# An adaLN transformer block on one Trainium2 core: one transfer for a slot in attention, SyncE in source order and residual rows loaded later in the feed-forward

## The chip, the cores and the metric

The kernel runs on one core of one Trainium2 chip. The metric is the device time of one execution in microseconds (us). Five engines with queues of their own work side by side: TensorE (PE, matrix products; PEld is its loading of weights), VectorE (DVE), ScalarE (ACT), GpSimd (POOL) and SyncE (SP, which here issues nearly all transfers and computes nothing). An engine takes the instructions of its queue in their order; between engines, semaphores make one wait for another. A transfer is carried out by the DMA engines and is behind the engine that issued it only in that this engine first waits until the transfer may start.

## The reference

One block of a transformer for 2048 rows of 512 fp32 numbers: attention with 32 query heads and 8 key heads of 128 over the last 512 keys of a cache, then a gated feed-forward of width 1792. Six vectors that come from one small product with the condition `c` shift, scale and gate both halves.

```python
def _A_ref(x, k_cache, v_cache, wq, wo):
    ...
    q = (x @ wq) ...                       # 32 heads of 128
    k = jnp.repeat(k_cache[:, :, Sk - W:, :], rep, axis=1)   # W = 512, rep = 4
    v = jnp.repeat(v_cache[:, :, Sk - W:, :], rep, axis=1)
    scores = jnp.einsum("bhqd,bhkd->bhqk", q, k) * (Dh ** -0.5)
    p = _softmax(scores, axis=-1)
    o = jnp.einsum("bhqk,bhkd->bhqd", p, v)
    return o ... @ wo

def _B_ref(x, w_gate, w_up, w_down):
    return (_gelu(x @ w_gate) * (x @ w_up)) @ w_down

mod = (_silu(c) @ w_mod).reshape(c.shape[0], 6, 1, -1)
...
h = _layernorm(x, axis=-1) * (1 + ca) + sa
x = x + ga * _A_ref(h, A_k_cache, A_v_cache, A_wq, A_wo)
h = _layernorm(x, axis=-1) * (1 + cb) + sb
x = x + gb * _B_ref(h, B_w_gate, B_w_up, B_w_down)
```

## The kernel before

**Arithmetic.** Every large fp32 product is made of three fp16 matmuls (`mm3`, L85 to L88): each operand is split into a high and a low fp16 tile, and low times high, high times low and high times high add up in one PSUM bank. The query projection and the feed-forward's first products are also done with seven block products in place of eight, so they read sums and differences of blocks of the input (the "combined blocks", loaded as `cb`) and of the weights. A set of such weights is four tiles, `w0`, `w1`, `w2` and `x3`.

**Attention** is written as a loop over T = 512 slots of 128 queries by 512 keys of one head. Four slots are a unit, sixteen a pair of heads (a group `g`, which starts at slot `t0`). Half 0, the first 256 slots, does query blocks 0 and 1 for all sixteen pairs, half 1 blocks 2 and 3. In a slot `t` TensorE makes the scores, VectorE their maximum (`peak`), ScalarE the exponentials (`expo`, L884); two slots later ScalarE writes the high part of the probabilities into a tile `p` (`high`, L896), three slots later VectorE the low part (`low`, L901), and `low` then has SyncE issue a DMA transpose of that tile (L905) into `pt`, which the product with `v` reads. There are four tiles `p` and three `pt`. Between these, TensorE works off a list of other tasks, three for each slot: query projections, products with `v`, and output rows `y`, which VectorE adds to one of eight accumulator tiles `acc` in SBUF (L852).

**Weights.** In half 0 the split tiles of `wq`, `k`, `v` and `wo` are made from raw fp32 loads, for the most part by GpSimd; each made tile is written to DRAM (`store`) and fetched again in half 1 (`fetch`, L315; both use DRAM tiles named `kept`). Half 1 prepares the feed-forward's weights in the same way, in staged tiles (`stage`) that share the five raw buffers (`prep_set`, `prep_wd`), and stores those for the feed-forward. Loads of raw tiles go through a list (`sched`): each has the slot in which its data is first used, is issued three slots earlier, and not before the buffer that it takes was released. The `xs` loads bring rows for the layer norm (raw buffers too; after attention these are the finished rows `y`), two `rw` buffers hold raw feed-forward weights.

**What sets the order.** The attention part, L1383 on, stands under `tc.manual_schedule()`: all engines keep the order of the source. At the end of a slot come `run(t)` (what was put at this slot: stores, fetches, reloads of accumulators), `run(("l", t))` (raw loads) and `run(("w", t))` (steps on loaded tiles). In before, the fetches of half 1 have fixed slots, four for a weight set at `t0 - 18` to `t0 - 15`, `k` at `t0 - 9`, `v` at `t0 + 1`, `wo` at `t0 + 12` and every second slot on. A transfer whose buffer is not yet free holds up SyncE and everything behind it, transposes included. `attn_final` (L858) stores a finished row and reloads its accumulator three slots later.

The feed-forward (L1437 on) runs over 28 chunks `q` of seven block products each, in the order 1, 2, 6, 7, 5, 4, 3; output rows `y` of the chunks before are worked in between (`y_next`). In before no manual order holds there: the framework's scheduler orders the instructions of each engine, SyncE's among them, by its own model of their durations. `f_final` (L1473) stores a row of the output and reloads the same accumulator at once for the row eight further on:

```python
def f_final(ti):
    nc.sync.dma_start(rows_of(out, ti), acc[ti])
    if ti < 2 * QT:
        load_acc(ti + 2 * QT, y1[ti + 2 * QT])
```

Of the kernel before, what the change touches and what calls it, by code (L numbers as in the profile page):

```python
# [63 lines left out]
def block_kernel(ctx: ExitStack, tc: tile.TileContext, x, kT, v, wq, wo, wg, wu, wd, cT, wc, wm, out):  # L64
# [35 lines left out]
    nc.sync.dma_start(cts, cT)  # L100
    for i in range(QT):
        load_acc(i, rows_of(x, i), nc.scalar if i < 2 else nc.sync)
# [32 lines left out]
    def mod_load(j, dt):  # L135
        t = raw("wmc")
        nc.sync.dma_start(t, wc[j, :, dt, :])
        return lambda: mod_col(j, dt, t, sbc)
# [171 lines left out]
    def store(key, t):  # L310
        KEPT[key] = dram.tile(list(t.shape), F16, name="kept")
        nc.sync.dma_start(KEPT[key], t)

    def fetch(key, t):
        nc.sync.dma_start(t, KEPT[key])  # L315
        return t
# [72 lines left out]
    def ln_out(qb, dt):  # L389
# [11 lines left out]
        def affine(act=True):  # L401
# [5 lines left out]
            nc.sync.dma_start(spilled(0, qb)[:, dt, :], st["f"])  # L407
# [12 lines left out]
    def ln_tile(gen, i, src):  # L420
# [4 lines left out]
        def load():  # L425
            st["x"] = raw("xs")
            nc.sync.dma_start(st["x"], src())
# [13 lines left out]
        def affine(dts):  # L441
# [7 lines left out]
            if KT - 1 in dts:  # L449
                nc.sync.dma_start(spilled(gen, qb)[:, :, i * P:(i + 1) * P], f.rearrange("p (k q) -> p k q", k=KT))  # L450
# [15 lines left out]
    def combos(gen, p, eng, base=True, d=0, e=0):  # L466
        X = {}

        def load(name):
# [5 lines left out]
            nc.sync.dma_start(X[name], stored(gen, name, p))  # L475
# [54 lines left out]
    def reader(src):  # L530
        st = {}

        def load():
            st["r"] = raw("raw")
            nc.sync.dma_start(st["r"], src)

        return st, load

    def wo_items(qd, ts_, tp):
        m = {}  # L540
        for k in range(4):
# [15 lines left out]
            if qd == 0:  # L557
                def load_kept(st=st, sp=sp, src=src):
                    st["r"] = sp["r"] = pool.tile([P, D], F32, tag="wo", name="wor", bufs=8)
                    nc.sync.dma_start(st["r"], src)  # L560
# [121 lines left out]
    def set_load(key, srcs, only=None):  # L682
        for k, src in enumerate(srcs):
            if only in (None, k):
                t = pool.tile([P, 512], F32, tag="rw", name="rw", bufs=NRW)
                nc.sync.dma_start(t, src)
# [224 lines left out]
    def early_load(j, dt):  # L911
        nc.sync.dma_start(wct[j][:, dt, :], wc[1, :, dt, :] if j else wm[0, dt])
# [132 lines left out]
    def gate_load(dt):  # L1045
        gps[dt] = raw("wmr")
        nc.sync.dma_start(gps[dt], wm[1, dt])
# [53 lines left out]
    for g in range(NG):  # L1101
# [136 lines left out]
    def prep_set(q, b):  # L1238
# [11 lines left out]
        def keep_it(k):  # L1250
            return lambda: store(("w", key, k), outs[k][0]["t"] if k < 3 else outs[k][0]["t"][:, :, 0:256])
# [25 lines left out]
    def prep_wd(n, b):  # L1277
# [3 lines left out]
        def load(k):  # L1281
            st[k] = raw("raw")
            nc.sync.dma_start(st[k], wd[(2 * n + k) * P:(2 * n + k + 1) * P, :])
# [19 lines left out]
        for k in range(2):  # L1303
            sched(b + 7 + 2 * k, (outs[k][1], [lambda k=k: make(k), lambda k=k: store(("wd", n, k), outs[k][0]["t"])]), b + 10 + 2 * k)
# [77 lines left out]

    with tc.manual_schedule():  # L1383
        begin()
        nexty = []
        for t in range(T + TAIL):
# [30 lines left out]
            run(("l", t))  # L1417
            run(("w", t))
            if t == T + 2:
# [23 lines left out]

    def y_next():
        if nexty:
            all_of(nexty.pop(0))

# [25 lines left out]
    def f_final(ti):  # L1473
        nc.sync.dma_start(rows_of(out, ti), acc[ti])
        if ti < 2 * QT:
            load_acc(ti + 2 * QT, y1[ti + 2 * QT])

    f_done = {(0, k) for k in ORDER} | {(1, 1), (1, 2), (1, 6)}
    for q in range(NQ):
        n, m = divmod(q, 2)  # L1480
        its = items(NG + q) if q < 2 else f_items(q)
        for k, pk in enumerate(ORDER):
# [3 lines left out]
            if k in (1, 2, 5, 6):  # L1486
# [43 lines left out]
```

## Time and profile before

| what | value |
|---|---|
| median of 3 runs | 1780.09 us (1779.77 to 1782.09) |
| the profiled execution, as a whole | 1783.9 us |
| its span in the profile | 1782.1 us, granted TensorE clock 0.998 of full speed |
| moved by DMA in the span | 329.71 MB, a mean of 185 GB/s; 80.0% of 16 engines' time in one queue |
| DMA transposes of `p` tiles | 512, a median of 3.6 us from issue to landing |
| fetches of kept weight tiles `w` and `wo` | 123 and 60 of 256 KB, 3.1 and 3.2 us |
| stores of staged and of `w` tiles | 56 and 39 of 256 KB, 3.5 and 3.3 us |

How the profile is read: one execution is recorded, instruction by instruction, and the profile gives for each engine the time in which it was busy, and for each instruction the idle time of its engine just before it, with what ended that idle time. In rows of the timeline the columns are the start in us, the duration, the engine, the line, the operation with the tiles it writes and reads, their shapes, and in square brackets the idle time before and what ended it. In rows by stretch the columns are the stretch, its length, then busy time and count of TensorE, its weight loads, VectorE, ScalarE and GpSimd, the granted clock, the busy share of the DMA engines and GB/s. In rows of waits: the engine, what released it, and the time. `SPq` is SyncE's own queue: the length of an instruction there is the time that issuing takes.

### The profile page before, as it was taken

The page shows a single profiled execution, that of the slowest core. Times are in us where ns is not written, and L with a number is a line of the kernel's source. Part 1 is how long each engine was busy: PE and PEld are TensorE (multiplying, and loading weights), DVE is VectorE, ACT ScalarE, POOL GpSimd, SP SyncE. Part 2 cuts the span into 40 slices and gives each one's busy share as a digit, 9 for nine tenths or more (in the row PEclk, how much of TensorE's full clock was granted, in tenths as well). Part 3 has the DMA queues.
Part 4 walks back from the last instruction along what each step waited for, and adds up shares of the span by engine and source line. Part 5 has one row for each costly group of instructions (what it writes and reads, how often), then busy time and mean ns, then how long its engine had stood idle before and what let it go on. Part 6 is the DMA issues. An engine that isn't in the chain of part 4 may idle for free.

```text
span 1782.1 us, 26030 instructions
## 1 busy us (share of the span) xinstructions
PE 1735.6 (97%) x8112; PEld 796.0 (45%) x8114; DVE 1442.5 (81%) x2517; ACT 1211.1 (68%) x2814; POOL 874.2 (49%) x1095
## 2 busy tenths in 40 slices
PE   7899999999999999999999999999999999999999
PEld 5444444444444444444444444444444444444444
DVE  7888888888888888888887888787885758676676
ACT  6877787878878777687877777777773455344342
POOL 4879878776788863236575375464420023000000
PEclk9999999999999999999999999999999999999999
DMA  7999999999999989999999999999985643252321
GB/s 232 197 189 236 204 224 207 222 214 206 218 211 210 211 175 182 228 223 212 217 208 211 237 203 212 212 196 203 187 184 141 215 126 99 73 177 84 86 69 56
DMA packets 663274, 329.71 MB, mean 185 GB/s; under 512 B 553184, under 2 KB 575968, under 8 KB 663136
## 3 DMA queue, kind: packets, MB, share of 16 engines
q1 hardware_dynamic: 662848, 327.53, 80.0%
q8 instruction: 64, 1.05, 0.3%
q14 instruction: 74, 0.61, 0.1%
q10 hardware_dynamic: 288, 0.52, 0.1%
HBM read 133.83 MB, written 59.90 MB: 109 GB/s over the span
## 4 chain that ended last, share of the span: by engine, by line
PE 67%; DVE 14%; ACT 7%; POOL 4%; DMA 4%; issue 4%; SPq 1%; POOLq 0%; ACTq 0%; DVEq 0%
PE py L86 7%; PE py L88 7%; PE py L87 7%; PE ps L86 4%; PE ps L88 4%; PE ps L87 4%; PE po L86 4%; PE po L88 4%; PE po L87 4%; DVE p L901 3%; DVE nm L875 3%; PE fa L86 2%; PE fa L88 2%; PE fa L87 2%; ACT ee L884 2%
## 5 line engine op out<-in xcount | busy, mean ns | idle before, releaser
L884 ACT ACTIVATE ee<-ps,nm 128x512 f32<-128x512 f32 x512 | 350.8, 685 | 244.6 <-DVE nm L875 234.6
L901 DVE SCALAR_TENSOR_TENSOR p<-ee,rr,p 128x512 f16<-128x512 f32 x512 | 464.8, 908 | 0.2
L875 DVE TENSOR_REDUCE nm<-ps 128x1 f32<-128x512 f32 x512 | 348.7, 681 | 67.2 <-PE ps L88 65.8
L896 ACT ACTIVATE p<-ee,rr 128x512 f16<-128x512 f32 x512 | 365.5, 714 | 12.8 <-DMA pt<-p 11.9
L86 PE MATMUL ps<-k,qt 128*128 128x512 f16 x512 | 194.3, 380 | 21.5 <-DVE qt L644 15.2
L86 PE MATMUL po<-pt,v 128*128 128x512 f16 x512 | 194.0, 379 | 2.8 <-DVE p L901 1.3
L86 PE MATMUL py<-wo,ot 128*128 128x512 f16 x512 | 194.1, 379 | 2.1 <-DVE ot L644 2.0
L88 PE MATMUL ps<-k,qt 128*128 128x512 f16 x512 | 194.2, 379 | 0.0
L87 PE MATMUL ps<-k,qt 128*128 128x512 f16 x512 | 194.2, 379 | 0.0
L88 PE MATMUL py<-wo,ot 128*128 128x512 f16 x512 | 194.0, 379 | 0.0
L87 PE MATMUL py<-wo,ot 128*128 128x512 f16 x512 | 194.0, 379 | 0.0
L88 PE MATMUL po<-pt,v 128*128 128x512 f16 x512 | 194.0, 379 | 0.0
L87 PE MATMUL po<-pt,v 128*128 128x512 f16 x512 | 194.0, 379 | 0.0
L892 DVE RECIPROCAL rr<-rr 128x2 f32<-128x2 f32 x256 | 41.5, 162 | 118.0 <-ACT rr L889 116.6
L87 PEld LDWEIGHTS <-w 128*128 128x128 f16 x728 | 71.4, 98 | 91.7 <-issue 7.6
L88 PEld LDWEIGHTS <-w 128*128 128x128 f16 x728 | 71.5, 98 | 86.8 <-issue 1.6
L86 PEld LDWEIGHTS <-w 128*128 128x128 f16 x728 | 71.4, 98 | 86.4 <-issue 1.3
L852 DVE SCALAR_TENSOR_TENSOR acc<-py,dysc,acc 128x512 f32<-128x512 f32 x112 | 81.7, 746 | 34.6 <-PE py L88 32.1
L362 POOL TENSOR_TENSOR rs<-rs,nhalf 128x1 f32<-128x1 f32 x32 | 19.2, 599 | 168.6 <-DVE rs L356 166.0
L884 ACT ACTIVATION_READ_ACCUMULATOR ee<-ps,nm 128x1 f32 x512 | 100.7, 197 | 0.0
L852 DVE SCALAR_TENSOR_TENSOR acc<-py,ysc,acc 128x512 f32<-128x512 f32 x128 | 94.6, 739 | 2.5 <-PE py L88 2.5
L86 PE MATMUL py<-wo,at 128*128 128x512 f16 x224 | 84.9, 379 | 3.0 <-DVE acc L852 1.9
(263 smaller groups left out, 3818.8 us busy)
## 6 DMA issues: line engine op xcount, KB each, us to landing
w<-kept SPq DMA_DIRECT2D x123, 256.0 KB, 3.1
wo<-kept SPq DMA_DIRECT2D x60, 256.0 KB, 3.2
raw<-in_wo SPq DMA_DIRECT2D x56, 256.0 KB, 3.5
kept<-stage SPq DMA_DIRECT2D x56, 256.0 KB, 3.5
kept<-w SPq DMA_DIRECT2D x39, 256.0 KB, 3.3
rw<-in_wq SPq DMA_DIRECT2D x38, 256.0 KB, 3.8
hs<-hf SPq DMA_DIRECT2D x32, 256.0 KB, 2.7
pt<-p SPq DMA_TRANSPOSE x512, 3.6
```

The costliest lines, as they stand in the source:

```text
L86: nc.tensor.matmul(ps, llo, rhi, start=first, stop=False, skip_group_check=chain)
L87: nc.tensor.matmul(ps, lhi, rlo, start=False, stop=False, skip_group_check=chain)
L88: nc.tensor.matmul(ps, lhi, rhi, start=False, stop=last, skip_group_check=chain)
L362: nc.gpsimd.tensor_tensor(st["rs"], st["rs"], nhalf, op=ALU.pow)
L852: nc.vector.scalar_tensor_tensor(acc[ti], st["p"], by, acc[ti], op0=ALU.mult, op1=ALU.add)
L875: nc.vector.tensor_reduce(nm, E[t]["ps"], axis=AX.X, op=ALU.max, negate=True)
L884: nc.scalar.activation(e, E[t]["ps"], AF.Exp, bias=E[t]["nm"], scale=1.0, accum_out=sm[:, t % 2:t % 2 + 1])
L892: return lambda: nc.vector.reciprocal(r, r)
L896: nc.scalar.activation(p16[:, 0, :], E[t]["e"], AF.Copy, scale=E[t]["r"])
L901: nc.vector.scalar_tensor_tensor(p16[:, 1, :], E[t]["e"], E[t]["r"], p16[:, 0, :], op0=ALU.mult, op1=ALU.subtract)
```

## The change

**Attention.** A function `dma` issues SyncE's transfers and counts them in `moved`, which is set back to nothing after each slot. Stores of half 0's tiles and the fetches of half 1 no longer have a fixed slot but a window: they are put on a list `bg` with the last slot by which they go (`store` with six slots of slack; `within` for the fetches). At the end of each slot, `spare` issues what is due on that list, and if no transfer was issued in this slot it takes the most urgent one from the list, or a raw load that may go already. Raw loads may be taken up to nine slots ahead of their use, three slots after their buffer was released. The stores of staged tiles have no slack and go at once, as do all stores of the last eight slots. One set of feed-forward weights and two `wo` tiles, which the feed-forward's second and first chunk fetched, are now fetched in the last slots of the attention part.

**Feed-forward.** The whole kernel stands under a manual schedule for SyncE, so its transfers keep the order of the source there too; the other engines are ordered by the scheduler as before. `f_final` no longer reloads the accumulator; it puts the row on a list `load_later`, and `y_next` reloads the first of the list once more than two are on it or no rows are left in `nexty`. While rows are on that list `y_next` is called after every block product and not after four of seven.

The replacement of `nc.sync.dma_start` by `dma` at the other places is left out of the diff below.

```diff
--- before.py
+++ after.py
...
-    acc = {}
-
-    def load_acc(i, src, eng=nc.sync):
+    acc, moved, bg = {}, [0], []
+
+    def dma(out_, in_):
+        moved[0] += 1
+        nc.sync.dma_start(out_, in_)
+
+    def load_acc(i, src, eng=None):
         acc[i] = pool.tile([P, D], F32, tag="acc", name="acc", bufs=2 * QT)
-        eng.dma_start(acc[i], src)
+        (eng.dma_start if eng else dma)(acc[i], src)
...
-    def store(key, t):
+    def store(key, t, slack=6):
+
         KEPT[key] = dram.tile(list(t.shape), F16, name="kept")
-        nc.sync.dma_start(KEPT[key], t)
+        if slack and 0 <= now[0] < T - 8:
+            bg.append((now[0] + slack, now[0], len(KEPT), lambda: dma(KEPT[key], t)))
+        else:
+            dma(KEPT[key], t)
+
+    def spare(t):
+
+        bg.sort(key=lambda x: x[:3])
+        while bg and bg[0][0] <= t:
+            bg.pop(0)[3]()
+        while not moved[0]:
+            may = [(x[0], 0, x[3], bg, x) for x in bg if x[1] <= t] + [(q[0][0], 1, q[0][2], q, q[0]) for q in pending.values() if q and q[0][1] <= t]
+            if not may:
+                break
+            _, _, fn, q, x = min(may, key=lambda x: x[:2])
+            q.remove(x)
+            fn()
+
+    def within(lo, hi, fn):
+        at(("w", max(lo, 0)), lambda: bg.append((hi, lo, 0, fn)))
 
     def fetch(key, t):
-        nc.sync.dma_start(t, KEPT[key])
+        dma(t, KEPT[key])
...
             st["x"] = raw("xs")
-            nc.sync.dma_start(st["x"], src())
+            dma(st["x"], src())
...
-        nc.sync.dma_start(y1[ti], acc[ti])
+        dma(y1[ti], acc[ti])
...
-            for k, pos in ((0, t0 - 18), (3, t0 - 17), (1, t0 - 16), (2, t0 - 15)):
-                at(pos, lambda g=g, pr=pr, k=k: set_fetch(g, pr, k))
+            for k, hi in ((0, 15), (1, 10), (2, 9), (3, 7)):
+                within(t0 - 18, t0 - hi, lambda g=g, pr=pr, k=k: set_fetch(g, pr, k))
         if half:
-            at(t0 - 9, lambda pr=pr: k_fetch(pr))
+            within(t0 - 14, t0 - 5, lambda pr=pr: k_fetch(pr))
             if pr % 2 == 0:
-                at(t0 + 1, lambda qd=qd: v_fetch(qd))
+                within(t0 - 6, t0 + 3, lambda qd=qd: v_fetch(qd))
                 for k in range(4):
-                    at(t0 + 12 + 2 * k, lambda h=4 * qd + k: wo_fetch(h))
+                    within(t0 + 4 + 2 * k, t0 + 22 + 2 * k, lambda h=4 * qd + k: wo_fetch(h))
...
-            return lambda: store(("w", key, k), outs[k][0]["t"] if k < 3 else outs[k][0]["t"][:, :, 0:256])
+            return lambda: store(("w", key, k), outs[k][0]["t"] if k < 3 else outs[k][0]["t"][:, :, 0:256], 0)
...
-            sched(b + 7 + 2 * k, (outs[k][1], [lambda k=k: make(k), lambda k=k: store(("wd", n, k), outs[k][0]["t"])]), b + 10 + 2 * k)
+            sched(b + 7 + 2 * k, (outs[k][1], [lambda k=k: make(k), lambda k=k: store(("wd", n, k), outs[k][0]["t"], 0)]), b + 10 + 2 * k)
...
-    for q, ps_ in ((0, (T - 18, T - 17, T - 16, T - 15)), (1, (T - 8, T - 7, T - 3, T))):
+    for k in range(2):
+        at(T - 1 + 2 * k, lambda k=k: WO.update({("f", 0, k): fetch(("wd", 0, k), get_wo())}))
+    for q, ps_ in ((0, (T - 18, T - 17, T - 16, T - 15)), (1, (T - 8, T - 7, T - 3, T)), (2, (T + 2, T + 3, T + 4, T + 5))):
         for k, pos in zip((0, 3, 2, 1), ps_):
             at(pos, lambda q=q, k=k: set_fetch(("f", q), ("f", q), k))
 
+    pending = {"raw": [], "rw": []}
     loads.sort(key=lambda l: l[0])
     released = {"raw": [0] * NRAW, "rw": [0] * NRW}
     for pos, (load, steps), kind, ahead in loads:
         assert len(pos) == len(steps), (pos, len(steps))
         go = pos[0] - ahead
-        go = max(go, released[kind].pop(0) + LDGAP)
+        free = released[kind].pop(0) + LDGAP
         released[kind].append(pos[-1])
-        at(("l", max(min(go, pos[0]), 0)), load)
+        pending[kind].append((max(min(max(go, free), pos[0]), 0), max(free + 3, pos[0] - 9), load))
...
+    ctx.enter_context(tc.manual_schedule(engines={mybir.EngineType.SP}))
     with tc.manual_schedule():
...
-            run(("l", t))
+            for q in pending.values():
+                while q and q[0][0] <= t:
+                    q.pop(0)[2]()
             run(("w", t))
+            spare(t)
+            moved[0] = 0
...
+    load_later = []
+
     def y_next():
         if nexty:
             all_of(nexty.pop(0))
+        if len(load_later) > 2 or load_later and not nexty:
+            t = load_later.pop(0)
+            load_acc(t, y1[t])
...
-    for n in range(2 * NP):
+    for n in range(1, 2 * NP):
         for k in range(2):
             f_at(2 * n + 1, 2 * k, lambda n=n, k=k: WO.update({("f", n, k): fetch(("wd", n % NP, k), get_wo())}))
-    for q in range(2, NQ):
+    for q in range(3, NQ):
...
     def f_final(ti):
-        nc.sync.dma_start(rows_of(out, ti), acc[ti])
+        dma(rows_of(out, ti), acc[ti])
         if ti < 2 * QT:
-            load_acc(ti + 2 * QT, y1[ti + 2 * QT])
+            load_later.append(ti + 2 * QT)
...
-            if k in (1, 2, 5, 6):
+            if k in (1, 2, 5, 6) or load_later:
                 y_next()
...
```

More of the change, by code (lines that the diff above doesn't have):

```diff
@@ L99, in block_kernel @@
     cts = const.tile([P, KT], F32, name="cts")
-    nc.sync.dma_start(cts, cT)
+    dma(cts, cT)
     for i in range(QT):
-        load_acc(i, rows_of(x, i), nc.scalar if i < 2 else nc.sync)
+        load_acc(i, rows_of(x, i), nc.scalar if i < 2 else None)
     ident = const.tile([P, P], F32, name="ident")
@@ L136, in mod_load @@
         t = raw("wmc")
-        nc.sync.dma_start(t, wc[j, :, dt, :])
+        dma(t, wc[j, :, dt, :])
         return lambda: mod_col(j, dt, t, sbc)
@@ L474, in load @@
                 X[name] = raw("cb")
-            nc.sync.dma_start(X[name], stored(gen, name, p))
+            dma(X[name], stored(gen, name, p))
         def diff(o, a, b):
@@ L534, in load @@
             st["r"] = raw("raw")
-            nc.sync.dma_start(st["r"], src)
+            dma(st["r"], src)
         return st, load
@@ L685, in set_load @@
                 t = pool.tile([P, 512], F32, tag="rw", name="rw", bufs=NRW)
-                nc.sync.dma_start(t, src)
+                dma(t, src)
                 RAW.setdefault(key, {})[k] = t
@@ L1046, in gate_load @@
         gps[dt] = raw("wmr")
-        nc.sync.dma_start(gps[dt], wm[1, dt])
+        dma(gps[dt], wm[1, dt])
     def gate_cols(dt):
```

10 lines of the change are left out of this document (5 added, 5 removed).

## Prediction

> **What bounds the kernel now.** I read the page first, then TensorE's busy time by stage, then the rows before which TensorE stood idle, and from each of them back to what it waited for.
>
> ```profile
> span 1782.1 us, 26030 instructions
> PE 1735.6 (97%) x8112; PEld 796.0 (45%) x8114; DVE 1442.5 (81%) x2517; ACT 1211.1 (68%) x2814; POOL 874.2 (49%) x1095
> 115.00:700.00 585.00, 581.06 (x2729) 264.58 (x2728) 509.03 (x902) 458.57 (x1133) 450.46 (x570) 1.00 0.94 207
> 700.00:1340.00 640.00, 629.77 (x2945) 286.05 (x2943) 537.60 (x958) 484.90 (x1178) 316.37 (x395) 1.00 0.96 210
> 1340.00:1500.00 160.00, 151.61 (x704) 69.33 (x703) 106.85 (x174) 72.04 (x135) 34.40 (x30) 0.99 0.50 147
> 1500.00:1750.00 250.00, 250.00 (x1160) 113.33 (x1159) 173.99 (x265) 100.69 (x158) 0.00 (x0) 1.00 0.32 95
> ```
>
> TensorE is busy for 1735.6 of 1782.1 us, and the change leaves its matmuls alone, so 46.5 us is all that any edit of transfers could win. The stages (length less TensorE's busy time, the first figure behind the length) say where it lies: 3.9 us from 115 to 700, 10.2 us from 700 to 1340 (attention's second half), 8.4 us where attention hands over to the feed-forward, nothing from 1500 to 1750. The rest, 24 us, is the head and the tail, whose instructions keep their order. The DMA engines are 0.94 and 0.96 busy in attention: there, when a transfer is issued decides when its neighbours land. In the feed-forward they are 0.32 busy.
>
> Attention's second half has these idle rows (in brackets: idle before, and what ended it):
>
> ```profile
> 841.96 0.38 PE L86 MATMUL ps<-k,qt 128*128 128x512 f16 x1 [0.97 <-ACT ee L884]
> 908.68 0.39 PE L86 MATMUL ps<-k,qt 128*128 128x512 f16 x1 [0.89 <-ACT p L896]
> 911.75 0.38 PE L86 MATMUL ps<-k,qt 128*128 128x512 f16 x1 [0.30 <-ACT ee L884]
> 978.43 0.38 PE L86 MATMUL po<-pt,v 128*128 128x512 f16 x1 [1.33 <-DVE p L901]
> 983.67 0.39 PE L86 MATMUL ps<-k,qt 128*128 128x512 f16 x1 [1.83 <-ACT p L896]
> 1152.92 0.38 PE L86 MATMUL po<-pt,v 128*128 128x512 f16 x1 [0.36 <-DMA pt<-p]
> 1233.15 0.38 PE L86 MATMUL ps<-k,qt 128*128 128x512 f16 x1 [1.62 <-ACT ee L884]
> ```
>
> They name ACT and DVE, but these had been waiting in their turn for transfers:
>
> ```profile
> 1223.22 1.23 SPq L905 DMA_TRANSPOSE pt<-p  x1
> 1224.50 0.58 SPq L315 DMA_DIRECT2D wo<-kept  x1
> 1225.12 0.44 SPq L315 DMA_DIRECT2D w<-kept  x1
> 1225.61 0.43 SPq L1283 DMA_DIRECT2D raw<-in_wd  x1
> 1231.62 0.63 ACT L212 ACTIVATE junk<-raw 128x512 f16<-128x512 f32 x1 [3.21 <-DMA raw<-in_wd]
> 976.01 0.32 SPq L427 DMA_DIRECT2D xs<-y  x1
> 980.53 0.69 DVE L352 BATCH_NORM_STATS2 bn<-xs 128x6 f32<-128x512 f32 x1 [2.19 <-DMA xs<-y]
> 978.37 0.72 ACT L896 ACTIVATE p<-ee,rr 128x512 f16<-128x512 f32 x1 [0.81 <-DMA pt<-p]
> ```
>
> The load of a `wd` tile is the third transfer of one slot; issued at 1225.61 it lets ACT go on at 1231.62, 6.0 us later. ACT stood 3.21 us, and TensorE then 1.62 us before 1233.15. Around 980 a residual tile and a transpose are late together.
>
> **The change part by part.** *One transfer a slot.* Counted in the order of instructions on SyncE, the stretches between two of the 512 transposes held no transfer 165 times, one 193, two 106, three 41 and four 6 times; now 33, 422, 44, 12 and 0. TensorE, VectorE, ScalarE and GpSimd keep attention's order exactly; nothing is added, and the transfers stay 772. SyncE's own time is relieved: a transpose takes 1.23 us of it and a transfer up to 0.58 (rows of 1223 to 1226), and a slot lasts about 1345 / 512 = 2.6 us, so four transfers (3.6 us) overrun a slot and one (1.8 us) doesn't. Attention's `wd` loads now stand six and two slots earlier for the pair of 1225; the fetches that shared slots with the residual loads of 908 and 980 have left. So the edit reaches the gaps 0.89, 0.30, 1.33, 1.83, 0.36 and 1.62, 6.3 us in all. It doesn't reach 0.97 at 841.96: that residual load waits for a staged store, which is stored at once before and after. I looked for what each moved fetch or store waits for (the buffer's last reader) in the rows of before: none is released later than its new place, so no new wait on SyncE is to be seen. Between nothing (a cure that only moves the wait) and 6.3, and with VectorE at 537.60 of 640 us too busy to pass on all of it, I take 3.8, three fifths. Cover: the fetch goes early, and its buffer must already be free; if it isn't, transposes behind it are late at once.
>
> A staged tile's store and the raw loads that wait for GpSimd stay where they are, and so does this wait:
>
> ```profile
> SPq L686 <- POOL stage L153: 22.6, 13, 3.1
> ```
>
> The Trainium skill's page "DMA: Bandwidth & Descriptors", section "Anatomy of one DMA", gives a transfer some 2.0 us fixed plus its bytes over 436 GB/s; for 256 KB my estimate from that is 2.6 us, and a transfer ahead would cost only 0.6 us. By it, two transfers cleared shorten a gap by 1.2 us at most and the 6.3 shrink to 5.2. The 6.0 us from issue to use at 1225.61 speaks against it here, where transposes share the queue; 2.6 us as a lone landing fits the median in the next rows.
>
> *The hand-over.* Here VectorE and ScalarE stand for loads (the second row is the total over the eight residual tiles, from the view of that tile between 1340 and 1500; then TensorE's rows; last the landing times of: the feed-forward's fetches after 1500, the stores of residual rows, and the residual tiles):
>
> ```profile
> 1354.08 0.69 DVE L352 BATCH_NORM_STATS2 bn<-xs 128x6 f32<-128x512 f32 x1 [3.74 <-DMA xs<-y]
>   DMA xs<-y: 14.1, 6
> 1402.38 0.69 DVE L352 BATCH_NORM_STATS2 bn<-xs 128x6 f32<-128x512 f32 x1 [3.59 <-DMA xs<-y]
> 1459.67 0.63 ACT L339 ACTIVATE b<-cb 128x512 f16<-128x512 f32 x1 [4.51 <-DMA cb<-hs]
> 1362.94 0.58 PE L86 MATMUL fa<-t,w 128*128 128x512 f16 x1 [2.33 <-ACT fg L785]
> 1404.64 0.38 PE L86 MATMUL py<-wo,at 128*128 128x512 f16 x1 [1.94 <-DVE acc L852]
> 1463.71 0.38 PE L86 MATMUL fa<-t,w 128*128 128x512 f16 x1 [0.82 <-ACT fu L785]
> 1478.49 0.38 PE L86 MATMUL fa<-b,w 128*128 128x512 f16 x1 [0.66 <-DVE fg L1178]
> DMA to landing us min/median/max: 1.9/2.6/5.4
> DMA to landing us min/median/max: 2.6/3.2/6.2
> DMA to landing us min/median/max: 2.6/3.0/5.3
> ```
>
> The planner had pulled the residual loads (`xs`) ahead, each behind the store of its own row: the first is issued at the very matmul after which VectorE wants it. In source order they stand behind all eight stores, and VectorE's statistics come later too: counted in matmuls between the issue's release and the place where VectorE stands, the room is 18, 18, 7, 30, 19, 18, 19 and 28, where it was 0, 12, 12, 12, 24, -4, 6 and 6. A matmul takes 250 / 1160 = 0.2155 us, so 18 are 3.9 us, over the median landing of 3.0. I take the 2.33 and 1.94 as gone: 4.3 us, bounds 0 and 4.3. For the combined blocks (`cb`) the least room before ScalarE's place was 3 matmuls in the first group and 0 in the second; now 15 and 6: of 0.82 + 0.66 I take 1.0, bounds 0 and 1.5.
>
> A new wait comes with it. The last of the eight accumulator reloads waits for the landing of the last row's store, and the first residual load and a weight fetch are queued behind it on SyncE:
>
> ```profile
> L852 DVE SCALAR_TENSOR_TENSOR acc<-py,dysc,acc 128x512 f32<-128x512 f32 x112 | 81.7, 746 | 34.6 <-PE py L88 32.1
> L315 SPq DMA_DIRECT2D w<-kept x51: 319/320/444, 1503.6 to 1739.9; - x51
> ```
>
> From that row's last matmul: 0.75 for the add, 3.2 for the store, two issues of 0.3, 3.0 for the load, so 7.6 us, then some 3 us of VectorE (four operations near 0.7) until a result that TensorE needs 49 matmuls = 10.6 us on. Just covered; with landings of 6.2 and 5.3 it is 5.3 us late. Bounds 0 and 5.3; I take 1.0, nearer the medians.
>
> *SyncE in source order after 1500, and the reloads a chunk on.* In before, the least room between a fetch's release and its first matmul is 37 matmuls (8.0 us). Now one fetch of a chunk's first weights stands behind a finished row's store, an accumulator reload and a `wo` fetch, released 25 matmuls = 5.4 us before its use; the next least is 34 (7.3 us). The 25: 0.75 + 3 x 0.32 + 2.6 = 4.3 us, covered; with the longest landing 5.4 it is 7.1, a loss of 1.7. As it is issued in a row with three others I take 0.9. The reloads themselves keep over 100 matmuls of room and cost nothing; that cover gone, they would cost their landing. Up to eight row products move ahead in two chunks without adding work.
>
> **The sum** against the profiled execution: 3.8 + 4.3 + 1.0 - 1.0 - 0.9 = 7.2 us, so a span of 1782.1 - 7.2 = 1774.9. That execution took 1783.9 us as a whole, the median of the three runs is 1780.09; the same 7.2 off gives **1772.9 us** as the median to be measured.
>
> **Rivals.** *The attention part yields nothing*: its lateness comes from GpSimd (22.6 us of SyncE's waiting, unchanged), or VectorE returns each gap a slot later. For it: 0.97 at 841.96 is such a case. Against: 1225.61 is a pure burst. Then -7.2 + 3.8 = -3.4: 1776.7 us.
>
> *No empty slots, slower*: the 165 transposes that met an empty queue are 33 now. If a transpose behind a transfer lands late enough, ScalarE waits for one of the four `p` tiles, as at 978.37, and TensorE after it. A late transpose costs between 0.36 (1152.92) and 0.89 (908.68), say 0.6; if one in eight of the 132 newly filled slots pays, that is 10 us, less the 3.4 of the hand-over: 1786.7. It decides from about one in twelve (11 x 0.6 = 6.8, more than the hand-over brings by 3.4). Against: 3.9 us of idle in the whole first half, where one-transfer slots were already the commonest.
>
> *Source order blocks SyncE*: the two new waits cost their upper bounds, 5.3 + 1.7, and the combined blocks bring nothing. Then 3.8 + 4.3 - 7.0 = 1.1 gained: 1779.0, no change.
>
> *All of it comes in full*: 6.3 + 4.3 + 1.5 and no new wait: 12.1, 1768.0.
>
> **How the numbers follow.** Chances: the forecast 0.43, all in full 0.14, attention yields nothing 0.14, source order blocks 0.11, no empty slots 0.18. Faster or slower counts from 0.2%, 3.6 us, what a measurement here can tell from no change. The forecast and the full case are faster, and over half of the attention rival, which sits at that bound: 0.64. The source-order case and the rest of the other are the same: 0.18. The no-empty-slots case is slower: 0.18. The range 1766 to 1784 leaves out over half of the slower case and, at the fast end, a share in which the small gaps go too; the forecast's own range is 1768 to 1777.
>
> **What would show it.** Right: ACT's wait before the `wd` statistics near 1231, VectorE's waits for `xs` (14.1 us after 1340) and ACT's 4.51 for `cb` shrink; TensorE's idle falls below 6.5 us from 700 to 1340 and below 5 us from 1340 to 1500, and 0 to 2 us appears near 1605, one fetch, after 1500. Wrong: idle from 700 to 1340 still near 10 us; ACT's `p` waiting for transposes all through; a wait for weights in every chunk after 1500; or the gaps of 115 to 700 growing.

## The result and the profile after

The changed kernel took 1768.47 us as a median of six runs (1767.02 to 1772.28), where the kernel before took 1781.57 us in six runs beside it (1779.77 to 1783.45). The ratio is 0.9929 with a 95% interval of 0.9918 to 0.994: 12.6 us of 1780 (10.7 to 14.6), where 7.2 had been forecast. The profiled execution took 1767.57 us, and its span was 16.3 us shorter than that of before. From the page of the changed kernel, the span and TensorE's part in its row of busy times:

```profile
span 1765.8 us, 25953 instructions
PE 1730.5 (98%) x8112; PEld 796.0 (45%) x8114; DVE 1442.3 (82%) x2517; ACT 1210.3 (69%) x2814; POOL 875.9 (50%) x1095
```

TensorE's idle time fell from 46.5 to 35.3 us. Its busy time fell by 5.1 us too, though it does the same matmuls: some of them ran slower before (below). The stretches by stage of the changed kernel, each cut at the same matmul as a stage of before (columns as in the prediction: stretch, length, TensorE busy, and so on):

```profile
113.50:697.20 583.70, 581.55 (x2731) 264.76 (x2730) 507.83 (x904) 459.25 (x1137) 452.67 (x571) 1.00 0.96 209
697.20:1330.20 633.00, 629.06 (x2946) 286.87 (x2945) 540.42 (x957) 483.74 (x1175) 314.88 (x393) 1.00 0.96 210
1330.20:1482.80 152.60, 149.22 (x705) 69.33 (x704) 103.56 (x172) 71.93 (x132) 27.83 (x26) 1.00 0.48 147
1482.80:1735.50 252.70, 250.89 (x1162) 113.47 (x1161) 177.65 (x266) 101.60 (x160) 6.53 (x5) 1.00 0.31 100
```

Length less busy time gives TensorE's idle time: 2.2 us in attention's first stage (3.9 before), 3.9 in its second half (10.2), 3.4 at the hand-over (8.4), and 1.8 after it, where there was none. So attention won 8.1 us, the hand-over 5.0, and the feed-forward gave 1.8 back. The same cut before and after for the first 455 matmuls, first before, then after:

```profile
5.00:115.20 110.20, 95.53 (x455) 50.64 (x458) 92.97 (x187) 84.69 (x198) 72.33 (x93) 0.98 0.89 219
```

```profile
5.00:113.50 108.50, 93.78 (x455) 50.25 (x458) 91.37 (x187) 83.99 (x197) 73.24 (x93) 1.00 0.90 224
```

Their idle time is the same 14.7 us; the granted clock is not, 0.98 against 1.00. This part is chance: in the profiles of e3, e7, e8 and e9, whose code up to there is that of the changed kernel, TensorE is busy for 95.3 to 97.4 us in the same stretch. It is one reason why the two profiled executions lie further apart than the medians.

**Attention.** ScalarE's group that writes the high part of `p`, from the groups by line (busy time, mean of one, idle before and what ended it), before and after:

```profile
L896 ACT ACTIVATE p<-ee,rr 128x512 f16<-128x512 f32 x512 | 365.5, 714 | 12.8 <-DMA pt<-p 11.9 <-DVE p L901 0.5 <-DVE rr L892 0.2
```

```profile
L920 ACT ACTIVATE p<-ee,rr 128x512 f16<-128x512 f32 x512 | 365.2, 714 | 1.7 <-DMA pt<-p 1.4 <-DVE rr L916 0.2
```

Waiting for late transposes shrank from 11.9 to 1.4 us over the whole span. From the end of VectorE's work on a tile `p` to the landing of its transpose took 4.55 us in the mean before and takes 4.17 now, although fewer transposes meet an empty queue. Most of that is SyncE's: it issues a transpose 0.52 us after VectorE is done where it took 0.77, while the time from issue to landing only went from 3.78 to 3.66. The `wd` load behind the gap of 1.62 us is now alone in its slot, and ScalarE reads its tile without a wait (timeline of SyncE, then of ScalarE, changed kernel):

```profile
1209.35 1.30 SPq L929 DMA_TRANSPOSE pt<-p  x1
1210.71 0.57 SPq L94 DMA_DIRECT2D raw<-in_wd  x1
1211.39 1.23 SPq L929 DMA_TRANSPOSE pt<-p  x1
...
1222.07 0.62 ACT L216 ACTIVATE junk<-raw 128x512 f16<-128x512 f32 x1
```

What is left in the second half at the places that the prediction listed, with the longest other pause (732.46) and the one at 1270.87:

```profile
732.46 0.38 PE L86 MATMUL ps<-k,qt 128*128 128x512 f16 x1 [1.03 <-ACT ee L908]
838.84 0.38 PE L86 MATMUL ps<-k,qt 128*128 128x512 f16 x1 [0.50 <-ACT ee L908]
905.47 0.39 PE L86 MATMUL ps<-k,qt 128*128 128x512 f16 x1 [0.50 <-DVE qt L668]
908.54 0.38 PE L86 MATMUL ps<-k,qt 128*128 128x512 f16 x1 [0.30 <-ACT ee L908]
977.97 0.39 PE L86 MATMUL ps<-k,qt 128*128 128x512 f16 x1 [1.00 <-ACT p L920]
1270.87 0.39 PE L86 MATMUL ps<-k,qt 128*128 128x512 f16 x1 [0.20 <-DVE qt L668]
```

Of the 6.3 us in reach, 0.50 + 0.30 + 1.00 are left: 4.5 are gone. The 0.97 that the prediction held out of reach is 0.50 now. The 1.03 was 0.39 before; in the traces of the kernels with the same attention it is anything from 0.54 to 1.03.

**Hand-over and feed-forward.** VectorE's waits for the residual tiles between 1330 and 1500 fell from 14.1 to 3.9 us (the view of that tile), and TensorE has these gaps of over 0.3 us after 1345:

```profile
  DMA xs<-y: 3.9, 4
...
1350.50 0.38 PE L86 MATMUL fa<-t,w 128*128 128x512 f16 x1 [0.69 <-ACT fg L809]
1432.08 0.39 PE L86 MATMUL fa<-b,w 128*128 128x512 f16 x1 [1.52 <-DMA w<-kept]
1574.53 0.38 PE L86 MATMUL fa<-t,w 128*128 128x512 f16 x1 [0.69 <-ACT u L809]
1576.67 0.38 PE L86 MATMUL fa<-t,x 128*128 128x512 f16 x1 [0.69 <-ACT u L809]
1578.56 0.39 PE L86 MATMUL fa<-b,w 128*128 128x512 f16 x1 [0.44 <-DMA w<-kept]
```

The 2.33 is now 0.69; the 1.94 and both gaps behind `cb` are gone; the last four rows are new. Two of them wait for a weight fetch, two for ScalarE to empty a PSUM bank.

### The profile page after: what moved, and what is told of

Same layout as the page of the kernel before. It is cut to its first block, busy times and chain, and to the rows that moved or that the text cites. A ratio compares the mean times of both kernels' runs of the same rounds, so it can differ in the third digit from the quotient of the medians.

```text
span 1765.8 us, 25953 instructions
## 1 busy us (share of the span) xinstructions
PE 1730.5 (98%) x8112; PEld 796.0 (45%) x8114; DVE 1442.3 (82%) x2517; ACT 1210.3 (69%) x2814; POOL 875.9 (50%) x1095
## 4 chain that ended last, share of the span: by engine, by line
PE 76%; DVE 11%; ACT 5%; POOL 3%; issue 3%; DMA 2%; SPq 0%; POOLq 0%; ACTq 0%; DVEq 0%
PE py L86 7%; PE py L87 7%; PE py L88 7%; PE ps L86 5%; PE ps L88 5%; PE ps L87 5%; PE po L86 4%; PE po L87 4%; PE po L88 4%; DVE p L925 3%; PE fa L86 3%; PE fa L88 2%; PE fa L87 2%; DVE nm L899 2%; PE qa L86 2%
## 5 line engine op out<-in xcount | busy, mean ns | idle before, releaser
L668 DVE SCALAR_TENSOR_TENSOR ot<-po,ot 128x512 f16<-128x512 f32 x128 | 86.9, 679 | 0.0
```

Of the source, the lines that this page charges most:

```text
L668: return lambda: nc.vector.scalar_tensor_tensor(t[:, 1, :], src, scale, t[:, 0, :], op0=ALU.mult, op1=ALU.subtract)
```

## The experiments

Each was timed against the kernel before on the same chip. Microseconds below are the ratio's difference from 1, times 1780; a comparison with the changed kernel sets two such ratios side by side.

| kernel | ratio to before, 95% interval | us against before |
|---|---|---|
| the change | 0.9929 (0.9918 to 0.994) | -12.6 |
| e1, attention's part alone | 0.9948 (0.9936 to 0.9961) | -9.3 |
| e2, feed-forward's part alone | 0.9988 (0.9977 to 0.9998) | -2.1 |
| e3, without SyncE's source order | 0.9951 (0.9938 to 0.9964) | -8.7 |
| e4, accumulators reloaded at once | 0.9978 (0.9968 to 0.9988) | -3.9 |
| e5, fetches at their old slots | 0.9978 (0.9967 to 0.9988) | -3.9 |
| e6, empty slots not filled | 1.0002 (0.9992 to 1.0012) | +0.4, no change |
| e7, row products spread | 0.9935 (0.9922 to 0.9949) | -11.6 |
| e8, weights fetched ahead of wo | 0.9918 (0.9903 to 0.9932) | -14.6 |
| e9, e7 and e8 together | 0.9918 (0.9903 to 0.9933) | -14.6 |
| e10, no raw load taken early | 0.9935 (0.992 to 0.995) | -11.6 |
| e11, every store at once | 0.9937 (0.9922 to 0.9951) | -11.2 |

### e1: attention's part alone

```diff
-    ctx.enter_context(tc.manual_schedule(engines={mybir.EngineType.SP}))
...
-    for n in range(1, 2 * NP):
+    for n in range(2 * NP):
...
-    for q in range(3, NQ):
+    for q in range(2, NQ):
...
-            load_later.append(ti + 2 * QT)
+            load_acc(ti + 2 * QT, y1[ti + 2 * QT])
...
```

> Attention as in the changed kernel, the feed-forward as before (SyncE ordered by the scheduler there, accumulators reloaded at once, the third weight set and the first two wo tiles fetched in the feed-forward). My theory now: attention's part is worth about 8 us and not the 3.8 of the prediction, because the rows before 1340 that I left out of the sum (1.20, 0.53 and smaller ones from 1249 to 1311) had the same cause. Then 1781.6 - 8 = 1773.6, TensorE idle from its 456th matmul to the feed-forward near 6 us where it was 14, and the hand-over still idle for 8 us with waits for xs. Rival, the prediction's size: -3.8, 1777.8, and the rest of the 13.1 us comes from the hand-over and the clock.

Median 1771.69 us beside 1779.88: -9.3 (6.9 to 11.4 by the interval). Two stretches of it, attention's second half and the hand-over, cut at the same matmuls as above:

```profile
698.30:1330.80 632.50, 629.02 (x2947) 286.95 (x2946) 541.24 (x957) 483.09 (x1175) 313.77 (x393) 1.00 0.96 211
1330.80:1488.40 157.60, 151.77 (x705) 69.60 (x704) 108.02 (x175) 72.91 (x135) 34.40 (x30) 0.99 0.48 148
```

The second half has 3.5 us of idle where before had 10.2. The hand-over has 5.8 where before had 8.4, although the feed-forward is that of before: the pause of 1.94 us is not in this trace, the 2.33 (2.17 here) and the two gaps behind `cb` are. The prediction's 3.8 lies outside this interval: attention was mis-sized.

### e2: the feed-forward's part alone

The edit puts into the kernel before what e1 takes out of the changed one.

```diff
+    ctx.enter_context(tc.manual_schedule(engines={mybir.EngineType.SP}))
     with tc.manual_schedule():
...
-            load_acc(ti + 2 * QT, y1[ti + 2 * QT])
+            load_later.append(ti + 2 * QT)
...
```

> Attention as before; SyncE in source order in the feed-forward, accumulators reloaded later, third set and first two wo tiles fetched early. My theory: the hand-over brings 5 us of idle and up to 1.5 of the slow clock behind the 2.33 us gap, and the new waits cost 3.6, so -3 to -5: 1777 to 1778.6. Rival (the feed-forward brings most of the gain): -9, 1772.6.

Median 1777.64 us, -2.1 (0.4 to 4.1), less than the 3 to 5 expected. With e1 that makes 11.4 of the 12.6: the two parts add up within their intervals, and about three quarters of the gain is attention's. The rival falls. By the traces the feed-forward's part would be worth more: in e2 the hand-over takes 152.2 us and what follows 252.9, where before had 160.4 and 250.4, which makes 5.7 us. The profiled execution of before, at 1783.9 us, was one of its slower ones, so stages taken from this one trace overstate gains.

### e3 and e4: the order on SyncE, and the late reloads

```diff
-    ctx.enter_context(tc.manual_schedule(engines={mybir.EngineType.SP}))
     with tc.manual_schedule():
```

> The changed kernel without the source order for SyncE in the feed-forward; all else stays, the later reloads too. My theory: the source order is what cures the waits for xs at the hand-over (about 6 us with the clock), against new waits of some 3 us that go with it here; so 3 us slower than the changed kernel, 1771.5, with gaps of about 2 us before the feed-forward's first products. Rival: the later reloads and early fetches do it, the order is worth nothing: 1768.5.

Median 1772.04 us; against the changed kernel 0.9951 to 0.9929, 3.9 us lost. In its trace the first of the hand-over's gaps is back:

```profile
1354.91 0.38 PE L86 MATMUL fa<-t,w 128*128 128x512 f16 x1 [2.50 <-ACT fg L809]
1355.12 0.38 PE L87 MATMUL fa<-t,w 128*128 128x512 f16 x1
```

The two gaps behind `cb` are back as well, with 0.94 and 0.66 us. So the source order is what cures these three, and neither the late reloads nor the early fetches do it without that. The pause of 1.94 us is gone here too, as in e1; what removed it the runs do not show.

```diff
     def f_final(ti):
         dma(rows_of(out, ti), acc[ti])
         if ti < 2 * QT:
-            load_later.append(ti + 2 * QT)
+            load_acc(ti + 2 * QT, y1[ti + 2 * QT])
...
-            if k in (1, 2, 5, 6) or load_later:
+            if k in (1, 2, 5, 6):
```

> The changed kernel with each accumulator reloaded right behind the store of its finished row, and row products only after four of the seven block products. My theory: in source order each of eight reloads holds SyncE until the store has landed (near 3 us), and the weight fetches of that chunk stand behind them with 25 to 37 matmuls (5 to 8 us) of room: 3 to 6 us slower than the changed kernel, 1771.5 to 1774.5, with TensorE waiting for w<-kept near 1570. Rival: the room covers it, and the two pauses of 0.69 us near 1575 go away because row products stay spread out: 1767.

Median 1777.03 us: by the ratios 8.7 lost against the changed kernel, more than expected. In its trace the 769 matmuls behind the hand-over take 173.9 us where the changed kernel's take 167.9. (e7 below puts the row products back and keeps the reloads late, and loses nothing that shows, so this is the reloads.) SyncE's waits between 1560 and 1600, its timeline, and TensorE's, all of e4:

```profile
SPq L94 <- DMA out_y<-acc: 22.3, 8, 3.7
...
1579.28 0.39 SPq L94 DMA_DIRECT2D out_y<-acc  x1
1582.46 0.32 SPq L94 DMA_DIRECT2D acc<-y  x1
1582.83 0.42 SPq L94 DMA_DIRECT2D wo<-kept  x1
1583.31 0.42 SPq L94 DMA_DIRECT2D w<-kept  x1
...
1586.95 0.61 PE L86 MATMUL fa<-b,w 128*128 128x512 f16 x1 [4.78 <-DMA w<-kept]
```

Eight times SyncE stands until an output row has been written, 2.8 us in the mean, and the weights are behind it: issued at 1583.31, needed 4.78 us before 1586.95. In the changed kernel the same view reads:

```profile
SPq L94 <- DMA out_y<-acc: 2.8, 2, 1.7
```

With source order but without the late reloads, only 3.9 of the 12.6 us are left; the list of reloads is its necessary partner.

### e5 and e6: what fills the slots

```diff
-            for k, hi in ((0, 15), (1, 10), (2, 9), (3, 7)):
-                within(t0 - 18, t0 - hi, lambda g=g, pr=pr, k=k: set_fetch(g, pr, k))
+            for k, pos in ((0, t0 - 18), (3, t0 - 17), (1, t0 - 16), (2, t0 - 15)):
+                at(pos, lambda g=g, pr=pr, k=k: set_fetch(g, pr, k))
...
-            within(t0 - 14, t0 - 5, lambda pr=pr: k_fetch(pr))
+            at(t0 - 9, lambda pr=pr: k_fetch(pr))
...
```

> The changed kernel with the fetches of half 1 (weight sets, k, v, wo) back at the fixed slots of before; the stores' slack, the early raw loads and the whole feed-forward stay. In the second half 77 stretches between transposes are then empty (20 in the changed kernel, 83 before). My theory: single file in the second half is what attention's gain comes from, so 5 to 7 us of it go: 1774 to 1776 where the changed kernel stands at 1768.5, with ScalarE's waits for transposes (pt<-p) back near 11 us. Rival: the gain comes from the raw loads taken early (wd, residual rows); then at most 1.5 us are lost, 1770.

```diff
+            moved[0] = 1
             spare(t)
```

> The changed kernel, in which a slot without a transfer takes none from the list: each store and fetch goes at the last slot of its window, raw loads three slots ahead as before. 148 stretches are empty (33 in the changed kernel, 165 before). My theory: bursts return, and with them the late transposes: 6 to 10 us slower than the changed kernel, 1775 to 1778. Rival (it is the new places of the fetches, away from the residual loads, that count, not the filling): within 2 us of the changed kernel, 1770.

e5 stands at 1776.54 us, by the ratios 8.7 over the changed kernel, somewhat more than expected; e6 at 1781.01, where all of the gain is gone, again more than expected. ScalarE's `p` group in e5 and then in e6 (groups by line):

```profile
L920 ACT ACTIVATE p<-ee,rr 128x512 f16<-128x512 f32 x512 | 365.4, 714 | 11.2 <-DMA pt<-p 10.5 <-DVE p L925 0.5 <-DVE rr L916 0.2
```

```profile
L920 ACT ACTIVATE p<-ee,rr 128x512 f16<-128x512 f32 x512 | 365.4, 714 | 12.3 <-DMA pt<-p 11.9 <-DVE rr L916 0.2 <-DVE p L925 0.2
```

Both have the late transposes of before again, one with the fetches at their old places, the other with new places but no filling. In the nine traces of kernels that have the fetches' windows and fill empty slots this wait is between 0.2 and 2.0 us, in the four that lack either (before, e2, e5, e6) between 10.5 and 12.8. The second half, where e5 differs from the changed kernel, takes 638.5 us in e5 and 637.7 in e6, against 633.0 in the changed kernel and 640.5 before.

The traces also show why the transposes are late. In the second half the 256 transposes wait for SyncE to issue them for 305 us in all before, 280 in e5, 316 in e6 and 216 in the changed kernel. From issue to landing they take 971, 955, 945 and 950 us. So e5 and e6 differ from the changed kernel in issuing alone: the transposes stand behind other transfers on SyncE, and do not land more slowly once issued.

Not all that e6 loses is lateness of transposes. Its tiles are fetched at the last slot of their window, and for two of them that is too late (TensorE's waits between 115 and 1340):

```profile
PE qa L86 <- DMA w<-kept: 1.4, 1, 1.4
...
PE ps L86 <- DMA k<-kept: 0.6, 1, 0.6
```

e5 has one of the gaps which the prediction had not counted among those that a transfer sets:

```profile
1277.34 0.39 PE L86 MATMUL ps<-k,qt 128*128 128x512 f16 x1 [1.10 <-DVE qt L668]
```

It names VectorE, as the 1.20 at this place before did. But e7 and e9, whose attention is the changed kernel's, have 0.97 and 0.94 at the same matmul, and e6 has 0.21, so the fetches' slots are not what decides it. e6 loses more than e5 in the head too, where its deferred stores go in bunches:

```profile
5.00:119.70 114.70, 98.78 (x456) 51.20 (x459) 90.89 (x185) 84.03 (x197) 72.00 (x93) 0.96 0.83 207
```

That is 6.2 us longer than the changed kernel's row for the head, and 3.8 longer than the longest in the profiles of e3, e4, e7, e8 and e9, whose head is the changed kernel's (108.9 to 110.9 us). So chance alone hardly explains it; how much of it is the deferring, one execution doesn't tell.

### e7, e8 and e9: the new waits in the feed-forward

```diff
-            if k in (1, 2, 5, 6) or load_later:
+            if k in (1, 2, 5, 6):
                 y_next()
+        while m == 1 and load_later:
+            t = load_later.pop(0)
+            load_acc(t, y1[t])
```

> The changed kernel with row products only after four of the seven block products throughout, and accumulators left on the list reloaded at the end of each pair of chunks. My theory: the two pauses of 0.69 us near 1575, in which a product waits for ScalarE to empty the bank fa, come from row products used up ahead, so that none stands between these products; they go: 1.4 us faster than the changed kernel, 1767.1. Rival: the pauses belong to the order of products itself and stay: 1768.5 or more, since reloads then come later.

The two pauses of 0.69 are gone, as the theory has it, but 0.80 us for a weight fetch came in their place, and the time is that of the changed kernel within the intervals (0.9935 and 0.9929): no gain shown.

```diff
-            f_at(2 * n + 1, 2 * k, lambda n=n, k=k: WO.update({("f", n, k): fetch(("wd", n % NP, k), get_wo())}))
+            f_at(2 * n + 1, 4 + k, lambda n=n, k=k: WO.update({("f", n, k): fetch(("wd", n % NP, k), get_wo())}))
...
-        for k, at_ in ((0, 2), (3, 2), (1, 3), (2, 4)):
+        for k, at_ in ((0, 1), (3, 1), (1, 2), (2, 3)):
```

> The changed kernel with each weight set of the feed-forward fetched one block product earlier, and its two wo tiles after the fifth and sixth product of a chunk in place of the first and third, so that they no longer stand ahead of the weights on SyncE. My theory: the waits for w<-kept go (1.52 us near 1432, where the fetch stood behind a wo fetch, and 0.44 near 1578): 1.5 to 2 us faster, 1766.7. Rival: fetched earlier they wait for their own buffer and hold up what is behind them, the residual loads at the hand-over first of all: 1769 to 1771.

> Weight sets of the feed-forward fetched one block product earlier and wo later (as in e8), and row products spread as in e7. My theory: e8 left 0.24 us of idle after 1500 and e7 took the two pauses of 0.69 away, which e8 took away as well, so nothing is left for the spreading: 1765.3, as e8. Rival: the two add up, 1763.9; or the later reloads at the end of the pair of chunks stand ahead of a weight fetch again, 1767.

In the changed kernel the fetch that TensorE waits for at 1432.08 is issued behind two `wo` fetches. All of these stand behind the store `hs<-hf`, for which SyncE waited 16.3 us until ScalarE had written `hf` (SyncE's timeline, then its waits between 1405 and 1432):

```profile
1425.39 0.52 SPq L94 DMA_DIRECT2D hs<-hf  x1
1426.34 0.33 SPq L94 DMA_DIRECT2D xs<-y  x1
1426.73 0.91 SPq L94 DMA_DIRECT2D wo<-kept  x2
1427.75 0.36 SPq L94 DMA_DIRECT2D w<-kept  x1
...
SPq L94 <- ACT hf L471: 21.1, 2, 16.3
SPq L94 <- PE py L88: 0.3, 1, 0.3
```

e8 takes the two `wo` fetches out of the way. Its `hs<-hf` is issued at 1427.00, still ahead of the weights, but the weight fetch follows at 1428.38, 1.4 us later and not 2.4, and TensorE no longer waits for it. A weight fetch ahead of that store was not tried. Its hand-over and feed-forward:

```profile
1331.50:1482.70 151.20, 149.04 (x705) 69.41 (x704) 104.81 (x172) 71.76 (x131) 28.58 (x26) 1.00 0.47 145
1482.70:1738.50 255.80, 255.56 (x1184) 115.72 (x1183) 178.50 (x271) 104.16 (x165) 6.12 (x5) 1.00 0.31 101
```

The hand-over is idle for 2.2 us and the feed-forward for 0.2, where it was 3.4 and 1.8; e9's feed-forward has none (TensorE busy for all of 258.2 us), but e9 ends level with e8 (0.9918 both). Both stand 2 us below the changed kernel by their ratios, and e8's trace has 2.8 us less of idle time in these two stages, though the intervals still overlap. They are the fastest versions of this study.

### e10 and e11: the two smaller parts of the filling

```diff
-            may = [(x[0], 0, x[3], bg, x) for x in bg if x[1] <= t] + [(q[0][0], 1, q[0][2], q, q[0]) for q in pending.values() if q and q[0][1] <= t]
+            may = [(x[0], 0, x[3], bg, x) for x in bg if x[1] <= t]
```

> The changed kernel without raw loads taken early into an empty slot (they go three slots ahead as before); windows for fetches and slack for stores stay. Empty stretches between transposes 54 (33 in the changed kernel). My theory: the fetches' windows alone clear the bursts (e5 lost 7 us without them, though raw loads could go early), so at most 1.5 us are lost: 1768.5 to 1770, ScalarE's waits for pt<-p under 4 us. Rival: the wd loads of 1225 come late again and with them 1.6 us and more: 1771 to 1772.

```diff
-    def store(key, t, slack=6):
+    def store(key, t, slack=0):
```

> The changed kernel with every store issued at once (no slack of six slots in half 0). Empty stretches 62, all of the more in the first half; stretches with two transfers 67 where they were 44. My theory: the first half has only 2 us of idle either way, so nothing measurable: 1768.5 to 1769.5. Rival: the stores' bursts delay transposes in the first 115 us, where TensorE's pauses also bring slow matmuls behind them: 3 us or more, 1771.5.

1770.16 and 1770.69 us, 1.1 and 1.4 above the changed kernel by the ratios, with intervals that overlap its own. That is what was expected of both, and ScalarE's waits for transposes in e10 are 2.0 us. Neither part is shown to matter by itself; e11's rival is not excluded by its interval, but its central value is under half of what that asked for. What it is worth that staged tiles are stored at once was not tried: a store of theirs that is put off can come to stand behind a load into the very buffer that it is to free.

## Why the prediction came out as it did

The direction, the mechanism in attention and the place of one new wait in the feed-forward held; the size did not. In attention it is SyncE's own time, which the prediction names, that the transposes gained. 7.2 us were forecast, 12.6 measured.

**Attention: mis-sized, 3.8 forecast (0 to 6.3), 9.3 measured in e1.** Of the six rows in reach three fifths were expected to go; 4.5 of 6.3 did, seven tenths, which is near. The step that failed is "the edit reaches the gaps 0.89, 0.30, 1.33, 1.83, 0.36 and 1.62, 6.3 us in all". From the row of 700 to 1340, and from that of 115 to 700, only the rows that could be followed by hand to one transfer were counted. What was left out and went: 2.0 of 2.2 us between 1249 and 1311, half of the 0.97 at 841.96, and 1.8 of the first stage's 3.9. The largest row between 1249 and 1311, in the kernel before:

```profile
1280.95 0.39 PE L86 MATMUL ps<-k,qt 128*128 128x512 f16 x1 [1.20 <-DVE qt L644]
```

It names VectorE. That it is a late transpose's delay, passed on and met again under another name, is possible but not shown: e7 and e9 have 0.97 and 0.94 there, with 1.5 us each of ScalarE's waits for transposes in their whole span. Whatever its cause, the bound should have been the stages' whole idle time, 14.1 us, and not the list.

**The hand-over: right in kind.** 4.3 forecast for `xs`; the 2.33 shrank to 0.69 and the 1.94 went, 3.6 together. For `cb` 1.0 was forecast, and the whole 1.5 went. e3 shows that the source order did this for the 2.33 and for `cb`; the 1.94 is gone in e1 and e3 too, without it. The wait at the eighth reload, put at 1.0 with 5.3 as its bound, is hardly to be found. The wait that did come, 1.52 us at 1432, had no term: in source order SyncE stands 16.3 us for a store that needs ScalarE, and the weights come behind it and behind two `wo` fetches. e8 moves those two fetches back, and the wait is gone.

**After 1500: the place right, the price half of it.** One fetch behind a finished row, a reload and a `wo` fetch was forecast at 0.9 (0 to 1.7); SyncE issues these four from 1572.65 to 1574.00, and the fetch cost 0.44. But the eight row products that "move ahead in two chunks without adding work" did add idle time: without them between two products into the same bank, TensorE twice waited 0.69 us for ScalarE. "That cover gone, they would cost their landing" held for the reloads: e4 lost 8.7 us.

**Sum of the feed-forward's terms:** 3.4 forecast, 2.1 measured in e2, inside its interval (0.4 to 4.1).

**The rivals.** No empty slots, slower: refuted by its own sign; ScalarE's waits for transposes fell by a factor of eight with fewer empty slots, and e6, which empties them again, loses the gain. (In its price, 11 x 0.6 is 6.6 and not 6.8, which changes nothing.) Attention yields nothing, because GpSimd's stage holds SyncE: refuted by e1. Source order blocks SyncE: its mechanism is real, as e4 shows, but the late reloads keep it from the changed kernel. All in full, 1768.0, is nearest in time and right for the wrong sum: it had 6.3 for attention, where 9.3 came, and no new wait, where 3.6 came (0.27 near 1381 by the trace, 1.52 and 1.81).

**The Trainium skill** ("DMA: Bandwidth & Descriptors", section "Anatomy of one DMA") had given 5.2 in place of the 6.3, which the sum did not use. What that section gives was fitted to transfers issued by GpSimd, and here SyncE issues them. As the rows outside the 6.3 made the difference, the runs do not decide between the two figures.

## What to carry to other kernels

Where one in-order queue holds small urgent transfers (here the transposes) between large ones, spread the large ones evenly and give each a window in place of a slot: e5 shows that the windows are needed, and e6, less cleanly, the filling of empty slots. The DMA engines were over nine tenths busy meanwhile; how much is to be had where they are not, no run here shows. Bound such a change by the whole idle time of the stage, since the engine named at a gap need not be its cause. An in-order issuing engine pays for every wait ahead of an urgent transfer, so put a reload that waits for a store's landing (e4), and fetches that are needed later (e8), behind the fetches that are needed next.

## What the hardware showed beside that

After some pauses TensorE's matmuls ran at half their rate for 3 us or a little more. In the kernel before, at the hand-over:

```profile
1362.94 0.58 PE L86 MATMUL fa<-t,w 128*128 128x512 f16 x1 [2.33 <-ACT fg L785]
1363.32 0.63 PE L87 MATMUL fa<-t,w 128*128 128x512 f16 x1
...
1366.17 0.38 PE L88 MATMUL fa<-t,w 128*128 128x512 f16 x1
```

Eight matmuls take 3.23 us from start to start, where eight of 0.2155 take 1.72: the pause of 2.33 cost 1.5 us more. The length of the pause alone does not decide it. In e1 a pause of 2.17 at the same place has it:

```profile
1352.52 0.38 PE L86 MATMUL fa<-t,w 128*128 128x512 f16 x1 [2.17 <-ACT fg L809]
1352.73 0.56 PE L87 MATMUL fa<-t,w 128*128 128x512 f16 x1
1353.08 0.63 PE L88 MATMUL fa<-t,w 128*128 128x512 f16 x1
```

The shortest single pause with it in these traces is one of 2.02 us in e11. In e3 one of 2.50 (its rows above) has not, and neither has this one of the changed kernel's head, which in e8 and e9 does have it:

```profile
86.25 0.39 PE L86 MATMUL ps<-k,qt 128*128 128x512 f16 x1 [2.39 <-DVE qt L668]
86.47 0.38 PE L87 MATMUL ps<-k,qt 128*128 128x512 f16 x1
```

The Trainium skill's page "TensorE: Matmul & The Clock Gate", section "Part 1: The HAM clock gate", has TensorE fall to half rate after an idle window of some 3.4 us that runs freely and is not started by the kernel. The half rate, the stretch of about 3 us and the chance in it agree with these rows; that the pause must fill such a window does not, since 2.17 us were enough. For such a kernel a pause over 2 us is thus worth about 1.5 us more than its length, some of the time, and the pauses in the head make single executions differ by a few microseconds: busy time of the first 455 matmuls was 93.78 us in the changed kernel's profile and 96.98 in e8's, whose head is the same code.
